# Another list of steps for a kernel of linear attention, a feed-forward layer and a soft mixture of experts

## The chip, the cores and the metric

The kernel runs on one core of one Trainium2 chip. The metric is the device time of one execution in microseconds (us); the median of three runs stands for a kernel. The engines of the core work in parallel: TensorE (PE in the profile; PEld is its loading of weights), VectorE (DVE), ScalarE (ACT), GpSimd (POOL) and SyncE (SP), which issues the DMA transfers. Each goes through its own instructions in order and waits at semaphores for the others.

## What is computed

Three layers follow each other, in fp32. The inputs are 4 batches of 768 tokens with 8 heads of 48 (so 3072 tokens of 384).

```python
# layer 1: linear attention with a decaying state
for t in range(S):
    cur = einsum('bhd,bhe->bhde', u[None] * kt, vt)
    y[:, :, t] = einsum('bhd,bhde->bhe', rt, state + cur)
    state = wt[:, :, :, None] * state + einsum('bhd,bhe->bhde', kt, vt)
# layer 2: x is y as 3072 x 384
h = x @ w_in                      # 384 x 2048
x = (h * cos(h)) @ w_out          # 2048 x 384
# layer 3: soft mixture of 8 experts with 4 slots each
logits = x @ phi                  # 384 x 32
d = softmax(logits, axis=0); slot_input = d.T @ x
for e in range(8):
    slot_out[e] = maximum(slot_input[e] @ w1[e], 0) @ w2[e]
out = softmax(logits, axis=1) @ slot_out
```

## The kernel before

The three layers are not run one after the other. The work is cut into some 1950 steps, and a string, `HEAD` (line 924), lists them by name with their numbers, as `rT.16` or `h.13.1`. A loop at line 710 goes through the string and calls each step's function; inside `manual_schedule` every engine carries out its instructions in the order in which the steps stand in the string. Semaphores see to the data: an engine whose next instruction isn't ready stands still, and everything behind it in its own order too. So the string sets the order on all five engines at once, and nothing else in the kernel does, up to the end of the list. Then a fixed piece of code follows (experts and outputs, lines 711 to 913), which the change leaves alone.

The families of steps that the text speaks of, with their engines and lines:

- **Attention**, 24 blocks of 128 tokens (the number after the name is the block). `lw lk lr lv lz` load on SP. `wT kT rT` transpose on TensorE, four 128x128 transposes each (L145). `wf` copies wT (ACT). `scan`, `sr`, `sp` (DVE, L160, L164, L168) make running products of w. `L` (DVE, L189, two halves) multiplies rT by them into the tile lt, `ks` (DVE, L195) multiplies kT. `kN` (TensorE, L213) transposes ks back, `ksn` (ACT, L236) copies it. `A` (L206) are 16 small matmuls of ks and lt (32 records in the trace: a small fp32 matmul leaves two), `mask` (DVE, L232) takes their half. `U` (L257) are 16 of ksn and v, `st` (DVE, L278) the state. `z` and `rz` scale and place the state, `y` (L289) makes the block's result in 32 small matmuls; `xh`, `xm`, `xc` split it into two parts for the next layer. wT, kT, rT, kN, A, U and y share three PSUM banks in turn, so that U can only be written when the bank that it gets has been read.
- **Feed-forward layer**, 96 units: token block t, quarter q. The weights are decoded in the first 60 us (`raw`, `q`, `abs`, `d2a`, `d2b`, `whi` and others). `h.t.q` is nine matmuls 128x512 on TensorE (L443 to L445). `turns` (ACT, L458), `rest` (DVE, L462), `cos` (ACT, L466) and `mul` (DVE, L471) make h cos(h) from it, in the tile g. It gets transposed by TensorE (`gT`, L478, four transposes, and the copy `gc`, L484) or by DMA (`gz`, `gd`, `gx`). `l.t.q` (L510) multiplies the result by the product of w_out and phi: four small matmuls that add to the logits of a group.
- **Slots**, 12 groups of two token blocks. `sum` and `lc` (TensorE, L523) give the group's logits, `max` (DVE, L531 to L536) their running maximum, `exp xt xr xd` the exponentials (the last group: `quart`, ACT, L542, four copies of a quarter each, and `exp`, ACT, L552), `dT` (L580) transposes them, `dc` (ACT, L587) copies one half into dt and `ltok` (DVE, L593) the other half into the tile ltok. `E.g.p` (L606) multiplies dt by the four g tiles of a token block, a matmul for each (in the last group, whose parts are halves of the columns, eight for each part); it uses the bank in which dT stood. `es` (DVE, L612) adds it to a running sum.
- **Weights of the experts**, 16 transfers of 1.5 MB on SP (`att`, `we`, `late0`).

The decode's and the attention's products need VectorE and ScalarE between two steps on TensorE again and again: rT, then L on VectorE, then A; kN, then ksn on ScalarE, then U; dT, then dc and ltok, then E. Such a way from TensorE to another engine and back is called a hand-over below. In the list, other steps of TensorE stand in between.

Of the kernel before, what the change touches and what calls it, by code (L numbers as in the profile page):

```python
# [928 lines left out]
abs.i.4 wT.2 L.1 d2b.i.4 y.0 q.i.5 d2a.i.5 wf.2 xh.0 kN.1 xm.0 ksn.1 scan.2 U.1 xc.0 lw.3 abs.i.5 st.1.0 h.0.0 d2b.i.5 z.1.1 q.o.0 d2a.o.0 whi.4 A.1
turns.0.0 st.1.1 abs.o.0 D.1 lv.2 rest.0.0 wn.4.0 h.0.1 lz.1 whi.5 rz.1.0 wn.4.1 mask.1 q.i.7 sr.2 raw.o.2 d2b.o.0 sp.2 wc.4.0 kT.2 wn.5.1 cos.0.0  # L930
wc.4.1 rz.1.1 rT.2 wc.5.1 ru.2 raw.o.1 mul.0.0 oT.1 q.i.6 oc.1 ks.2 lk.3 L.2 abs.i.7 wT.3 wn.5.0 d2a.i.7 lr.3 turns.0.1 wf.3 lr.4 wc.5.0 z.2.0 kN.2
ksn.2 d2b.i.7 lk.4 abs.i.6 y.1 xh.1 U.2 d2a.i.6 whi.7 gT.0.0 rest.0.1 st.2.0 scan.3 z.2.1 sr.3 d2b.i.6 xm.1 xc.1 wn.7.0 lv.3 q.o.1 wn.7.1 gc.0.0
cos.0.1 sp.3 wc.7.1 h.1.0 mul.0.1 wc.7.0 abs.o.1 bo.2 rz.2.1 lw.4 abs.o.2 turns.1.0 rT.3 oT.0 d2a.o.1 st.2.1 d2b.o.1 h.0.2 bs.2 oc.0 whi.6 rest.1.0
turns.0.2 raw.o.3 D.2 L.3 A.2 lz.2 q.o.2 wn.6.0 kT.3 mask.2 gT.0.1 wT.4 cos.1.0 rest.0.2 ks.3 wc.6.0 d2a.o.2 lv.4 rz.2.0 wf.4 raw.o.4 mul.1.0 oT.2 y.2
q.o.3 ru.3 xh.2 oc.2 kN.3 xm.2 bo.3 ksn.3 d2b.o.2 A.3 xc.2 oT.3 gc.0.1 oT.5 bs.3 oc.3 D.3 h.1.1 z.3.0 scan.4 d2a.o.3 cos.0.2 abs.o.3 oc.5 lr.5 raw.o.5
wn.6.1 turns.1.1 lw.5 oT.4 oc.4 om.0 mask.3 sr.4 wc.6.1 rest.1.1 rz.3.0 mul.0.2 d2b.o.3 lz.3 abs.o.4 q.o.4 pc.0 U.3 cos.1.1 st.3.0 kT.4 lv.5 h.0.3
ks.4 z.3.1 oT.7 d2a.o.4 oT.6 st.3.1 gT.0.2 oc.7 d2b.o.4 kN.4 oc.6 ksn.4 mul.1.1 rT.4 sp.4 oT.8 om.1 turns.0.3 oc.8 wT.5 abs.o.5 rest.0.3 pT.0 wf.5
ps.0 cos.0.3 h.1.3 q.o.5 pc.1 oT.9 oc.9 turns.1.3 L.4 mul.0.3 d2a.o.5 z.4.0 lw.6 raw.o.7 ru.4 lk.5 U.4 d2b.o.5 st.4.0 gc.0.2 q.o.7 l.0.0 pT.1 rest.1.3
h.1.2 rz.3.1 oT.11 ps.1 gT.0.3 z.4.1 turns.1.2 scan.5 oT.10 oc.11 raw.o.6 rest.1.2 lw.7 bo.4 l.0.1 cos.1.3 ru.5 oc.10 abs.o.7 y.3 st.4.1 om.2 A.4 sr.5
xh.3 wT.6 cos.1.2 gc.0.3 mul.1.3 bs.4 abs.o.6 lz.4 sp.5 D.4 d2a.o.7 h.2.0 gT.1.1 xm.3 q.o.6 mul.1.2 pc.2 d2b.o.7 wf.6 mask.4 h.2.1 oT.14 turns.2.0  # L940
pT.2 gc.1.1 d2a.o.6 rz.4.1 xc.3 oT.15 rz.4.0 ps.2 oc.15 gT.1.0 oc.14 d2b.o.6 close lr.6 l.0.2 rT.5 oT.13 oT.12 gc.1.0 lk.6 gT.1.2 oc.13 bo.5 ru.6
rest.2.0 L.5 cos.2.0 l.1.0 l.1.1 y.4 mul.2.0 oc.12 z.5.0 gc.1.2 xh.4 om.3 kT.5 bo.6 xm.4 pc.3 gT.1.3 pT.3 h.2.2 turns.2.1 lz.5 scan.6 lr.7 rest.2.1
ps.3 sr.6 ks.5 cos.2.1 rT.6 kN.5 gc.1.3 l.1.2 xc.4 sp.6 l.1.3 lz.6 turns.2.2 ksn.5 mul.2.1 L.6 bs.5 l.0.3 sum.0 bs.6 A.5 U.5 rest.2.2 lc.0 rz.5.0 D.5
h.2.3 mask.5 max.0 D.6 gT.2.0 lk.7 st.5.0 lv.6 cos.2.2 exp.0 wT.7 z.5.1 mul.2.2 turns.2.3 kT.6 xt.0 lr.8 xr.0 lw.8 rest.2.3 ks.6 gc.2.0 cos.2.3 st.5.1
mul.2.3 h.3.0 kN.6 xd.0 wf.7 scan.7 h.3.2 turns.3.0 rest.3.0 dT.0 ksn.6 sr.7 U.6 cos.3.0 z.6.0 dc.0 ltok.0 l.2.0 E.0.0 gT.2.1 st.6.0 mul.3.0 rz.5.1
lv.8 lw.9 z.6.1 h.3.1 wT.8 sp.7 turns.3.2 gc.2.1 rest.3.2 ru.7 cos.3.2 turns.3.1 st.6.1 lv.7 mul.3.2 A.6 rest.3.1 mask.6 gT.2.2 h.3.3 gz.3.2 kT.7 wf.8
rz.6.1 l.2.1 cos.3.1 y.5 gz.3.0 gc.2.2 bo.7 bs.7 mul.3.1 rz.6.0 ks.7 gd.3.2 xh.5 rT.7 h.4.1 gd.3.0 xm.5 gz.3.1 lk.8 scan.8 L.7 turns.3.3 sr.8
turns.4.1 xc.5 rT.8 rest.3.3 D.7 kN.7 sp.8 cos.3.3 E.0.1 ksn.7 mul.3.3 rest.4.1 y.6 xh.6 wT.9 wf.9 cos.4.1 h.4.0 L.8 mul.4.1 turns.4.0 xl.6 ru.8
# [115 lines left out]
```

## Time and profile before

| | |
|---|---|
| median of 3 runs (lowest to highest) | 482.76 us (482.46 to 484.51) |
| the profiled execution | 482.29 us, its span 480.5 us |
| busy share: PE, PEld, DVE, ACT, POOL | 94%, 72%, 84%, 74%, 25% |
| mean granted clock of TensorE | 0.993 of full speed |
| chain that ended last: PE, DVE, ACT, DMA | 74%, 11%, 5%, 4% |
| largest group: h matmuls (L443 to L445), 3 x 288 | 121.9 + 112.6 + 113.2 us in records |
| transfers of expert weights (16 of 1.5 MB) | median 9.3 us from issue to landing |

The span runs from the first to the last instruction; 1.8 us of the profiled execution's time lie around it. A busy TensorE isn't TensorE at its peak: matmuls are pipelined and their records overlap, so that the sum of the records of a group can be more than the time that passes. A line of the timeline gives the start, the duration, the engine, the line of the kernel, the operation, the tiles (out<-in) and in brackets the idle time of the engine before it and what ended it. Runs of the same instruction stand in one line with their count; the duration is then that of the run.

### The profile page before, as it was taken

What the parts mean: (1) busy time and instruction counts of PE and PEld (TensorE: products, weight loads), DVE (VectorE), ACT (ScalarE), POOL (GpSimd) and SP (SyncE); (2) the same over time, 40 slices, a digit from 0 to 9 for tenths busy, and PEclk for the clock granted to TensorE, in tenths of its full rate; (3) what the DMA queues carried; (4) which work ended last, traced back from release to release, by engine and by line L of the source; (5) the groups of instructions that cost most, each with busy time, mean ns of one, the idle gap of its engine ahead of it and who ended that gap; (6) DMA issues with size and microseconds to landing.
All of it is one profiled execution on the core that took longest, in us unless ns stands there. A gap on an engine that the chain in (4) does not pass through costs nothing.

```text
span 480.5 us, 15374 instructions
## 1 busy us (share of the span) xinstructions
...
## 2 busy tenths in 40 slices
...
GB/s 214 309 297 211 171 211 208 59 74 84 139 199 127 162 173 139 153 193 172 140 158 158 204 157 177 188 120 149 179 135 130 233 256 411 247 337 405 368 125 272
DMA packets 205589, 94.21 MB, mean 196 GB/s; under 512 B 181840, under 2 KB 187216, under 8 KB 205520
## 3 DMA queue, kind: packets, MB, share of 16 engines
...
## 4 chain that ended last, share of the span: by engine, by line
PE 74%; DVE 11%; ACT 5%; DMA 4%; SPq 3%; issue 1%; POOL 0%; ACTq 0%; POOLq 0%
PE h L443 12%; PE h L445 11%; PE h L444 11%; PE l L510 5%; PE E L606 4%; PE y L289 4%; PE gT L478 4%; PE A L206 3%; PE U L257 3%; PE hps L797 2%; PE so L834 2%; PE wT L145 2%; PE kT L145 2%; DVE g L462 2%; PE rT L145 2%; PE kN L213 2%
## 5 line engine op out<-in xcount | busy, mean ns | idle before, releaser
L443 PE MATMUL h<-wu,x 128*128 128x512 f32 x288 | 121.9, 423 | 0.2
L445 PE MATMUL h<-wu,x 128*128 128x512 f32 x288 | 113.2, 393 | 0.0
L444 PE MATMUL h<-wu,x 128*128 128x512 f32 x288 | 112.6, 391 | 0.0
L466 ACT ACTIVATE g<-g,half_pi 128x512 f32<-128x512 f32 (+1 forms) x97 | 69.5, 720 | 17.0 <-DVE g L462 16.0
L458 ACT ACTIVATE g<-h 128x512 int32<-128x512 f32 (+1 forms) x96 | 57.1, 595 | 32.9 <-PE h L445 25.0
L471 DVE TENSOR_TENSOR g<-g,h 128x512 f32<-128x512 f32 x96 | 64.7, 676 | 9.0 <-ACT g L466 8.1
L462 DVE SCALAR_TENSOR_TENSOR g<-g,h 128x512 f32<-128x512 int32 (+1 forms) x96 | 64.7, 675 | 8.6 <-ACT g L458 7.7
L443 PEld LDWEIGHTS h<-wu,x 128*128 128x128 f32 x288 | 54.3, 189 | 18.2 <-DVE g L471 2.3
L445 PEld LDWEIGHTS h<-wu,x 128*128 128x128 f32 x288 | 54.0, 188 | 12.3
L444 PEld LDWEIGHTS h<-wu,x 128*128 128x128 f32 x288 | 54.4, 189 | 8.7
L220 POOL TENSOR_SCALAR_AFFINE_SELECT lt<-bo 64x512 f32<-64x512 f32 x48 | 38.0, 793 | 68.1 <-ACT bo L248 57.7
L492 ACT COPY zg<-g 128x1024 uint16<-128x1024 uint16 x51 | 52.8, 1042 | 1.8 <-DVE g L471 1.2
L267 POOL TENSOR_TENSOR z<-st_state,qt 128x192 f32<-128x192 f32 x35 | 22.0, 629 | 118.3 <-DVE st_state L278 94.2
L173 POOL TENSOR_TENSOR ru<-rn,u_b 128x384 f32<-128x384 f32 x24 | 26.1, 1086 | 81.5 <-DVE bo L243 32.1
L275 ACT COPY rzs<-z 64x192 f32<-64x192 f32 x96 | 33.4, 348 | 1.4 <-DVE z L263 0.4
L232 DVE COPY_PREDICATED lt<-cs,A 64x256 f32<-64x256 uint32 x72 | 32.2, 447 | 1.9 <-PE A L206 0.4
L189 DVE TENSOR_TENSOR lt<-rT,pt 64x512 f32<-64x512 f32 x48 | 32.8, 684 | 0.8 <-PE rT L145 0.3
L168 DVE TENSOR_TENSOR_SCAN pt<-wf,ini_f 128x520 f32<-128x520 f32 x24 | 30.9, 1289 | 0.0
L160 DVE TENSOR_TENSOR_SCAN qt<-wf,one_b 128x520 f32<-128x520 f32 x24 | 29.8, 1242 | 0.0
L289 PEld LDWEIGHTS y<-lt,rzs 128*32 128x32 f32 x1536 | 23.5, 110 | 6.2 <-issue 3.7
L174 POOL TENSOR_TENSOR ru<-ru,kn 128x384 f32<-128x384 f32 x24 | 26.9, 1120 | 2.0 <-DMA kn<-in_k_dram 0.2
L478 PE MATMUL gT<-cs,g 128*128 128x128 f32 x180 | 27.1, 275 | 0.0
...
## 6 DMA issues: line engine op xcount, KB each, us to landing
...
```

The lines of the kernel that those rows point to most:

```text
L220: nc.gpsimd.affine_select(out=lt[j % 2][h, a], in_=bo_t[j][h, a].unsqueeze(2).to_broadcast([64, NS, C]), pattern=[[0, NS], [-1, C]], compa ...
L275: nc.scalar.copy(rzs[j % 2][64 * a:64 * a + 64, c, :, a, RZ[a]], z_t[j, c][64 * a:64 * a + 64])
L289: nc.tensor.matmul(ps[m:m + 32, o, c * C:(c + 1) * C], lhsT=rz[:, c, p, a, 32 * b:32 * b + 32], rhs=L[:, a, 2 * p + c, :], start=m not in ...
L443: nc.tensor.matmul(half[:, f], lhsT=xh[:, c, :], rhs=wh, start=(c == 0), stop=False)
L444: nc.tensor.matmul(half[:, f], lhsT=xl[:, c, :], rhs=wh, start=False, stop=False)
L445: nc.tensor.matmul(half[:, f], lhsT=xh[:, c, :], rhs=wl, start=False, stop=(c == KD - 1))
L458: nc.scalar.activation(gt.bitcast(I32), hp, AF.Copy, bias=0.25, scale=1.0 / TWO_PI)
L462: nc.vector.scalar_tensor_tensor(out=gt, in0=gt.bitcast(I32), scalar=-TWO_PI, in1=hp, op0=ALU.mult, op1=ALU.add)
L466: nc.scalar.activation(gt, gt, AF.Sin, bias=half_pi[:, 0:1])
L471: (nc.gpsimd if pool else nc.vector).tensor_tensor(out=gt, in0=gt, in1=hp, op=ALU.mult)
L478: nc.tensor.transpose(ps[:, m * 128:(m + 1) * 128], gt[:, m * 128:(m + 1) * 128], ident)
L492: copy(zg, g_t[t, q].bitcast(U16).rearrange("p (f i) -> p i f", i=2))
```

## The change

Only the string `HEAD` differs: the same steps, each as often as before, in another order. No step's code, no tile and no transfer is added, removed or resized; the order of the two engines' accesses to a tile may differ where the steps stand the other way round. The whole of the string's lines is replaced; one of the old and one of the new, from around block 23 of the attention, show what such a line is:

```diff
 HEAD = """
...
-rest.20.1 cos.20.1 cmb.2.2 mul.20.1 rest.20.0 gT.20.1 turns.20.2 kN.23 l.19.0 rest.20.2 l.19.1 l.19.2 z.23.0 ksn.23 cos.20.2 l.19.3 L.23 sum.9 U.23
...
+turns.20.2 gc.19.3 rz.23.0 rT.23 gT.20.1 rest.20.2 l.19.0 l.19.1 ksn.23 rest.20.0 l.19.2 l.19.3 cos.20.2 L.23 U.23 mul.20.2 sum.9 gc.20.1 cos.20.0
...
```

Three places on TensorE, as the two orders have them. In the names, the number behind the last underscore is a tile's running number and means nothing else. A fourth place needs no rows: gT8_3, the transposes of unit (8, 3), stood one h step ahead of dT3 and now stands between dT3 and rT12, so that before E3 come dT3, gT8_3, rT12 and l of unit (8, 0), and in the old list dT3, rT12 and that l.

TensorE before U of attention block 16, at about 264 to 268 us, before and after (nine rows of h13_1 are left out in each but for the first and the last).

```order
L213 MATMUL kN16_4198<-cs_105,ks16_4162 128x128 x4
L145 MATMUL rT16_4214<-cs_105,rn0_119 128x128 x4
L145 MATMUL kT17_4219<-cs_105,kn1_122 128x128 x4
L443 MATMUL h13_1_4237<-wu1_322,x01_116 128x512
...
L445 MATMUL h13_1_4237<-wu1_322,x01_116 128x512
L580 MATMUL dT5_4247<-cs_105,dl1_114 128x128
L257 MATMUL U16_0_4251<-vn0_125,ksn16_4224 64x48
```

```order
L145 MATMUL rT16_4196<-cs_105,rn0_119 128x128 x4
L213 MATMUL kN16_4205<-cs_105,ks16_4179 128x128 x4
L443 MATMUL h13_1_4212<-wu1_323,x01_116 128x512
...
L445 MATMUL h13_1_4212<-wu1_323,x01_116 128x512
L580 MATMUL dT5_4231<-cs_105,dl1_114 128x128
L145 MATMUL kT17_4235<-cs_105,kn1_122 128x128 x4
L257 MATMUL U16_0_4246<-vn0_125,ksn16_4210 64x48
```

kT17 moved from before h13_1 to behind dT5, and rT16 and kN16 changed places.

TensorE at the end of the list, from the last group's logits (lc11) to the second half of its E, before and after.

```order
L523 MATMUL lc11_6715<-lg11_6713,cs_105 128x256
L606 MATMUL E10_6580<-g21_0_6301,dt10_6566 32x512
L606 MATMUL E10_6580<-g21_1_6394,dt10_6566 32x512
L606 MATMUL E10_6580<-g21_2_6280,dt10_6566 32x512
L606 MATMUL E10_6580<-g21_3_6172,dt10_6566 32x512
L580 MATMUL dT11_6743<-cs_105,dl1_114 128x128
L606 MATMUL E11_1_6750<-g22_0_6482,dt11_6745 32x256
```

```order
L523 MATMUL lc11_6714<-lg11_6712,cs_105 128x256
L580 MATMUL dT11_6729<-cs_105,dl1_114 128x128
L606 MATMUL E10_6578<-g21_0_6306,dt10_6567 32x512
L606 MATMUL E10_6578<-g21_1_6330,dt10_6567 32x512
L606 MATMUL E10_6578<-g21_2_6284,dt10_6567 32x512
L606 MATMUL E10_6578<-g21_3_6171,dt10_6567 32x512
L606 MATMUL E11_1_6746<-g22_0_6458,dt11_6736 32x256
```

The second half of E10 moved behind dT11. In the same stretch the steps quart.11 and max.11 (ScalarE and VectorE, both readers of the bank of lc11) changed places in the list.

TensorE before U of attention block 23, at about 384 us, before and after: the rows from the transposes of rT23 to U (h20_2 cut to its first and last row; of U's rows one).

```order
L145 MATMUL rT23_6034<-cs_105,rn1_120 128x128 x4
L443 MATMUL h20_2_6041<-wu2_468,x01_116 128x512
...
L445 MATMUL h20_2_6041<-wu2_468,x01_116 128x512
L510 MATMUL l9_6000<-gx18_2_6039,p_sb_109 32x128 x4
L510 MATMUL l9_6000<-gt18_3_5927,p_sb_109 32x128 x4
L478 MATMUL gT20_1_6075<-cs_105,g20_1_6055 128x128 x4
L213 MATMUL kN23_6082<-cs_105,ks23_6020 128x128 x4
...
L257 MATMUL U23_0_6113<-vn1_126,ksn23_6102 64x48
```

```order
L478 MATMUL gT19_3_6035<-cs_105,g19_3_5857 128x128 x4
L510 MATMUL l9_5951<-gx18_2_6033,p_sb_109 32x128 x4
L510 MATMUL l9_5951<-gt18_3_5993,p_sb_109 32x128 x4
L213 MATMUL kN23_6064<-cs_105,ks23_6001 128x128 x4
L145 MATMUL rT23_6076<-cs_105,rn1_120 128x128 x4
L478 MATMUL gT20_1_6081<-cs_105,g20_1_6046 128x128 x4
...
L257 MATMUL U23_0_6109<-vn1_126,ksn23_6095 64x48
```

rT23 moved from ahead of h20_2 to behind it, behind two l and kN23.

## Rows read from the trace of the kernel before

**Rows 1.** Stretches: length, PE, PEld, DVE, ACT, POOL busy (instructions), PEclk, DMA share, GB/s.

```profile
9.70:60.00 50.30, 44.80 (x549) 31.91 (x549) 48.78 (x73) 44.70 (x83) 14.55 (x14) 1.00 1.03 244
60.00:420.00 360.00, 358.02 (x5030) 279.10 (x5028) 327.26 (x649) 281.78 (x579) 97.79 (x117) 1.00 0.79 171
```

**Rows 2.** Timeline of TensorE at 209 us: start, duration, line, operation, tiles, count.

```profile
209.50 0.60 PE L145 MATMUL wT<-cs,wn 128*128 128x128 f32 x4
210.03 0.69 PE L206 MATMUL A<-lt,ks 64*64 64x64 f32 x32
210.65 0.50 PE L443 MATMUL h<-wu,x 128*128 128x512 f32 x1
210.99 0.40 PE L444 MATMUL h<-wu,x 128*128 128x512 f32 x1
211.22 0.40 PE L445 MATMUL h<-wu,x 128*128 128x512 f32 x1
```

**Rows 3.** Timelines of TensorE and VectorE around U of block 16.

```profile
264.51 0.60 PE L145 MATMUL rT<-cs,rn 128*128 128x128 f32 x4
264.95 0.60 PE L145 MATMUL kT<-cs,kn 128*128 128x128 f32 x4
265.30 0.48 PE L443 MATMUL h<-wu,x 128*128 128x512 f32 x1
...
267.67 0.31 PE L257 MATMUL U<-vn,ksn 64*64 64x48 f32 x2
268.50 0.68 PE L257 MATMUL U<-vn,ksn 64*64 64x48 f32 x30 [0.52 <-DVE lt L189]
269.41 1.07 PE L606 MATMUL E<-g,dt 128*32 128x512 f32 x8 [0.24 <-ACT dt L587]
...
266.97 1.39 DVE L189 TENSOR_TENSOR lt<-rT,pt 64x512 f32<-64x512 f32 x2
```

**Rows 4.** Timeline of TensorE before E of group 3.

```profile
205.58 0.42 PE L510 MATMUL l<-gx,p_sb 128*32 128x128 f32 x8
206.32 1.07 PE L606 MATMUL E<-g,dt 128*32 128x512 f32 x8 [0.31 <-DVE ltok L593]
```

**Rows 5.** Timelines of TensorE and VectorE around U of block 23.

```profile
378.77 0.60 PE L145 MATMUL rT<-cs,rn 128*128 128x128 f32 x4
...
381.38 0.42 PE L510 MATMUL l<-gx,p_sb 128*32 128x128 f32 x8
381.62 0.40 PE L510 MATMUL l<-gt,p_sb 128*32 128x128 f32 x8
...
383.99 1.10 PE L257 MATMUL U<-vn,ksn 64*64 64x48 f32 x32
...
382.98 1.39 DVE L189 TENSOR_TENSOR lt<-rT,pt 64x512 f32<-64x512 f32 x2
```

**Rows 6.** Timeline of VectorE at the start: its second decode step.

```profile
8.94 0.96 DVE L356 SCALAR_TENSOR_TENSOR qi<-rawi,qi 128x768 int32<-128x768 int32 x1 [1.19 <-ACT qi L346]
```

**Rows 7.** Timelines of TensorE, VectorE and ScalarE at the end of the list.

```profile
430.43 0.70 PE L523 MATMUL lc<-lg,cs 128*128 128x256 f32 x2 [0.55 <-DVE lg L517]
431.06 1.06 PE L606 MATMUL E<-g,dt 128*32 128x512 f32 x8
433.44 0.33 PE L580 MATMUL dT<-cs,dl 128*128 128x128 f32 x1 [1.32 <-ACT dl L552]
434.27 1.93 PE L606 MATMUL E<-g,dt 128*32 128x256 f32 x32 [0.51 <-ACT dt L587]
...
432.04 0.42 DVE L531 TENSOR_REDUCE mx<-lc 128x1 f32<-128x256 f32 x1 [1.67 <-ACT dl L542]
...
431.16 0.84 ACT L542 COPY dl<-lc 32x64 f32<-32x64 f32 x4 [0.36 <-PE lc L523]
```

**Rows 8.** Stretches at the end of the list and after the last matmul, columns as in rows 1.

```profile
432.50:433.00 0.50, 0.00 (x0) 0.00 (x0) 0.31 (x2) 0.06 (x1) 0.00 (x0) 1.00 0.99 393
474.25:474.50 0.25, 0.00 (x0) 0.00 (x0) 0.00 (x0) 0.00 (x0) 0.00 (x0) 0.50 1.04 295
```

More of the change, by code (lines that the diff above doesn't have):

```diff
@@ L929 @@
[L929 to L948, printed above, removed]
@@ new lines @@
+y.4 oc.13 om.3 cos.2.0 xh.4 z.6.0 lv.5 mul.2.0 pc.3 scan.6 kT.5 gT.1.2 ks.5 pT.3 bs.5 turns.2.1 ru.6 h.2.2 gc.1.2 lk.7 gT.1.3 rest.2.1 rz.5.0 ps.3
+sr.6 turns.2.2 gc.1.3 lr.7 bo.6 kN.5 rT.6 sp.6 xm.4 D.5 rest.2.2 ksn.5 cos.2.1 l.1.2 l.1.3 l.0.3 L.6 A.5 xc.4 mul.2.1 sum.0 U.5 lv.6 lc.0 mask.5
+cos.2.2 h.2.3 max.0 st.5.0 mul.2.2 exp.0 turns.2.3 gT.2.0 xt.0 rest.2.3 kT.6 gc.2.0 xr.0 xd.0 ks.6 wT.7 h.3.0 gT.2.1 cos.2.3 mul.2.3 lr.8 ru.7 z.5.1
+dT.0 kN.6 wf.7 scan.7 turns.3.0 ksn.6 lk.8 st.5.1 lv.7 ltok.0 h.3.2 dc.0 bs.6 rest.3.0 sr.7 lz.5 U.6 E.0.0 rz.6.0 bo.7 cos.3.0 st.6.0 gc.2.1 mul.3.0
@@ new lines @@
+l.3.2 turns.4.2 rz.7.0 st.7.0 rest.4.2 gz.4.0 cos.4.2 z.7.1 lr.10 l.3.3 scan.9 mul.4.2 lk.10 sum.1 gd.4.1 st.7.1 h.5.0 rz.7.1 z.8.0 ru.10 lc.1 A.8
+kN.8 lz.8 lk.9 turns.5.0 lw.11 max.1 exp.1 rest.5.0 mask.8 ksn.8 cos.5.0 mul.5.0 xt.1 h.4.3 gd.4.0 sr.9 lw.10 xr.1 gz.4.2 gx.4.0 U.8 kT.9 xd.1
+turns.4.3 ks.9 h.5.1 gz.5.0 dT.1 kN.9 rest.4.3 st.8.0 cos.4.3 bo.10 ltok.1 dc.1 y.7 z.8.1 E.1.0 mul.4.3 l.4.0 ru.9 bs.10 xh.7 rz.8.1 st.8.1 lv.9 z.9.0
+wT.10 gd.4.2 turns.5.1 sp.9 gd.5.0 h.5.2 ksn.9 rest.5.1 bo.9 xl.7 wf.10 U.9 cos.5.1 mul.5.1 gT.4.3 rT.9 lw.12 gx.5.0 gx.4.2 st.9.0 turns.5.2 rest.5.2
```

154 lines of the change are left out of this document (83 added, 71 removed).

## The prediction

> **What bounds the kernel now.** I read the stretches first, then TensorE's order in time, then what VectorE and ScalarE did at the places where TensorE stood. The stretches [rows 1]: between 60 and 420 us TensorE is busy for 358.02 of 360.00 us, VectorE for 327.26, ScalarE for 281.78. TensorE bounds this stretch, three quarters of the kernel. Its busy time is not quite its work, however: the records of neighbouring matmuls overlap, so what counts is the distance from one start to the next. Inside an h step (nine matmuls) starts are 0.23 us apart in records of 0.39 to 0.40 us [rows 2], the same wherever I looked. Hence a stall first eats the overlap, unseen, and shows as idle time only afterwards. Going through the starts of 60 to 420 us one by one and comparing each with the usual distance of its kind, I find 9.6 us above the usual, 5.6 us of it at places that lose over 0.15 us each, against 1.98 us of idle time in [rows 1]. That is all that a better order can win there, unless the distances themselves change.
>
> The Trainium skill, page "Perfetto Trace Analysis", section "Identifying the Most-Contended Engine", says that matmul busy time is a poor measure, and that the share of weight loading and the occupancy of the other engines are to be compared. By it TensorE has 279.10 of 360.00 us [rows 1], below VectorE's 327.26, so that VectorE would bound and a list that spares TensorE would bring nothing: the time would stay at 482.8. The even 0.23 us between starts speaks against it here; it stands beside the first rival.
>
> **The change, part by part.** The instructions of each engine are the same; only their order differs.
>
> *Distances.* Four transposes take 0.35 us until an h step starts (264.95 to 265.30), 0.44 until four other transposes (264.51 to 264.95) [rows 3] and 0.53 until small fp32 matmuls such as A (209.50 to 210.03) [rows 2]. An h step takes about 0.10 longer before small matmuls than before transposes (2.25 to 2.27 against 2.16 us, over the 15 such pairs of the trace). Counted in the two lists: transposes before small matmuls 61 to 29 (32 x -0.18 = -5.8 us); transposes before transposes 46 to 67 (21 x +0.09 = +1.9); h before small ones 15 to 44 (29 x +0.10 = +2.9); the other kinds stay within a dozen with distances that are about equal. Sum -1.0 us; with distances as they scatter, -0.6 to -1.4.
>
> *Hand-overs, 60 to 420 us.* Two places show what one costs. E of group 3: TensorE transposes dT, then rT, does an l step at 205.58 and starts E only at 206.32 [rows 4], 0.74 us later, where an l step usually takes 0.24 (381.38 to 381.62 [rows 5]): 0.5 us lost, of which 0.31 are idle. E needs both readers of dT to be done (dt on ScalarE, ltok on VectorE), and only rT and l stand between. The new list puts the four transposes of gT8_3 there too, 0.35 to 0.44 us of work: the loss goes but for about 0.1. U of block 16: it starts at 267.67, stalls 0.52 us for the product lt of VectorE (L189), and E follows at 269.41 [rows 3]; a step of the kind usually takes 0.62 (A, 210.03 to 210.65 [rows 2]), so 1.74 - 0.62 = 1.1 us are lost. Here rT16 was transposed at 264.51, but VectorE came to it at 266.97. So VectorE's queue was late, not TensorE. The new list moves kT17 from before h13_1 to just before U (0.44 us of cover) and takes one 0.2 us reciprocal out of VectorE's queue, but E still waits for the same chain lt, ltok, dt. I count -0.3 of the 1.1 us.
> All places together: with the work on TensorE between a hand-over's two ends minus the time of the middle instruction as cover, 25 of 187 hand-overs of the old list have under 0.5 us, and 13 of 190 of the new one. Half of the 5.6 us would be -2.8; E of group 3 gives back nearly all and U16 a third, so I take -2.0. Ends: 0 (VectorE's queue decides everywhere, as at U16) and -4 (all but the waits on late queues go).
>
> *Start, to 60 us.* VectorE is busy for 48.78 of 50.30 us from 9.7 on, TensorE for 44.80 [rows 1]: VectorE bounds here. The list moves z0 and the second decode step ahead, into the 1.19 us that VectorE stood idle until 8.94 [rows 6]. But the scan that comes next on it needs the first wT from TensorE and wf from ScalarE in any case, so that most of the gain is only moved behind. I take -0.5; ends -2.8 (the VectorE work that the new order takes from before the third token block's first h) and +1.0 (wT1 now stands before kT0 and rT0, so that ks and lt of block 0 come later).
>
> *End, 420 to 437 us.* In the old list ScalarE copies the last logits in four quarters (0.84 us from 431.16), and only then VectorE takes the maximum, at 432.04, though it was idle for 1.67 us [rows 7]; dT follows at 433.44. In the new list the maximum (0.42) goes first and the quarters behind it, while the 0.3 us of VectorE that follow the maximum run beside them: dT about 0.45 us earlier. But E10's second half (1.06 us, 431.06), which filled the wait for dT, now stands behind dT, where it fills the 0.83 us from dT to E11 (433.44 to 434.27) and overruns it by a few tenths. Together -0.1; ends -0.5 and +0.4.
>
> *Weights.* The transfers of expert weights (16 of 1.5 MB, 9.3 us from issue to landing by the table) stand in both lists in nearly the same place, the last five in another sequence. I cost it at 0, since the output stage uses them one after the other and none is due at once; without that cover the one that is moved to the end would be late by up to the fifth of 9.3 us that five of them share out, +2.
>
> Sum: -1.0 - 2.0 - 0.5 - 0.1 = -3.6 us on the profiled execution's 482.29 us: 478.7. The profiled execution lies 0.47 below the median of the runs shown (482.76), so the forecast is **479.2 us**. This kernel's measurement can tell about 0.5%, 2.4 us, from no change: faster is below 480.35, slower above 485.2.
>
> **Rivals.**
> 1. *The hand-overs bring nothing*, because VectorE's queue, not TensorE's list, is late wherever TensorE stands, as at U16 (lt 2.5 us after its rT started [rows 3]). Then the distances, 1.0 us, are all: 482.76 - 1.0 = 481.8. For it: VectorE busy 327.26 of 360 [rows 1]. Against: E of group 3.
> 2. *VectorE's queue before lt: slower.* The new list transposes rT later. Block 23 is the clearest place: rT was at 378.77, lt at 382.98, U at 383.99 [rows 5]; now rT stands behind h, l and kN, 1.3 us of TensorE's work before U, less than the 1.39 us of the two halves of lt alone. Seven blocks have under 0.9 us of cover before the one that needs lt or its bank, three before. If VectorE is not free just then, each waits for its queue: U16 shows 1.9 us from the end of rT (264.51 + 0.60) to lt; less about 0.5 of cover, 1.4 us each. Four more such places: +5.6, and the hand-overs' -2.0 are then not there either: -1.6 + 5.6 = +4.0, **486.8**. It decides from three places on (+2.6). Against: at block 23 VectorE reached lt at 382.98 anyway, about when the new rT ends, and the old list's three places lost some 0.3 us in all.
> 3. *The clock falls at the end.* Between the last logits and dT TensorE stood idle for 1.32 us and kept the granted clock of 1.00, 2.4 GHz (row of 432.50 to 433.00) [rows 7, 8]. Without E10 in between it stands about 1.9 us. After its very last matmul the row of 474.25 to 474.50 has 0.50, 1.2 GHz, with no matmul in it [rows 8]. If the clock falls, E10's half and E11 (1.06 + 1.93 us [rows 7]) take up to twice as long: +2.5, so 481.7.
> 4. *The start follows VectorE wholly* (-2.8 instead of -0.5): 476.9.
> 5. *Weights late* by 2 us: 481.2.
>
> The Trainium skill, page "TensorE: Matmul & The Clock Gate", part 1, has the clock released by recent activity and gated after idleness; the rows at the end agree, and it is the third rival's mechanism. The rows of 431 to 434 us show that an idle stretch nearly as long left the clock alone, so the rival stays a rival.
>
> **How the numbers follow.** Forecast (479.2, itself 477 to 481) 0.40; rival 1 0.17; rival 2 0.17; rival 3 0.12; rival 4 0.09; rival 5 0.05. Faster by over 0.5%: rival 4 and all of the forecast but the sixth that lies above 480.35, 0.43. Slower: rival 2, 0.17. The same: the rest, 0.40. The range leaves out a tenth on either side: low 475.5, since the ends of the middle (-4), the distances (-1.4) and the start (-2.8) hardly come together; high 485.5, within rival 2.
>
> **What would show it.** In the changed profile: the start of the last dT minus the start of the last logits, 2.6 us instead of 3.0, with quarters behind the maximum; E of group 3 starting without idle time; U16's stall still there but under 0.5 us; TensorE's idle time from 60 to 420 us under 1.5 us, and that stretch of work some 3 us shorter. Rival 2 shows as TensorE waiting for lt (L189) at blocks 3, 6, 10 and 23; rival 3 as a granted clock below 1.00 around 435 us and E11 records of 3 us and more. I am wrong if the sum of TensorE's waits in the middle grows, or if an h step follows another by over 2.16 us where nothing is idle.

## The result, and the profile after

The changed kernel takes 490.4 us (median of 4 runs, 488.35 to 491.4) against 482.66 us for the kernel before: 1.0141 times as long, with a 95% interval of 1.0116 to 1.0166. The forecast was 479.2 us and faster. Its profiled execution has a span of 489.1 us, 8.6 more than before.

Three readings of TensorE split these 8.6 us: the start of the first group's logits, of the last group's, and of the column sums behind the last E (all lc at L523, the sums at L765).

| | before | after | difference |
|---|---|---|---|
| first logits | 100.91 | 105.59 | +4.7 |
| from the first to the last logits | 329.52 | 331.06 | +1.5 |
| from the last logits to the column sums | 5.92 | 8.25 | +2.3 |
| from there to the end of the span | 44.15 | 44.20 | 0.0 |

So in this execution the start loses most, the middle, where the gain was to come from, loses too, and the end loses as much as a rival had said. One execution is one draw, however. The experiments below leave parts of the list as they are, and their profiled executions show how far such a reading goes without any change. The end of the new list took 5.59 to 8.25 us in seven kernels, its middle 329.91 to 332.18 us in eight, and its first logits came at 104.69 to 105.70 us in four. The old list's end took 5.92 us in three kernels and its middle 329.52 to 329.88 us in five.

The stretches of the kernel after, columns as in [rows 1]:

```profile
9.70:60.00 50.30, 42.16 (x470) 30.62 (x471) 46.83 (x66) 40.47 (x77) 14.64 (x14) 1.00 1.06 247
60.00:420.00 360.00, 356.48 (x5069) 275.85 (x5068) 326.16 (x635) 281.73 (x577) 94.15 (x117) 1.00 0.77 164
57.00:58.00 1.00, 0.00 (x0) 0.00 (x0) 0.94 (x3) 0.45 (x1) 0.90 (x1) 1.00 0.86 332
60.00:61.00 1.00, 1.00 (x6) 1.00 (x5) 0.00 (x0) 0.75 (x2) 0.00 (x0) 0.50 0.11 29
438.00:439.00 1.00, 0.00 (x0) 0.00 (x0) 0.42 (x3) 0.93 (x6) 0.00 (x0) 0.73 0.87 296
440.00:441.00 1.00, 1.00 (x8) 0.20 (x4) 0.45 (x2) 0.14 (x1) 0.00 (x0) 0.50 1.00 406
```

The first row stands against 44.80 us of TensorE in [rows 1], 549 matmul records against 470: the same stretch does less. The third and the fourth are one event: TensorE idle for a whole microsecond, and then busy at a granted clock of 0.50, that is 1.2 GHz. The last two are another of the same kind.

**The end.** Timelines of TensorE, VectorE and ScalarE, against [rows 7]:

```profile
436.65 0.70 PE L523 MATMUL lc<-lg,cs 128*128 128x256 f32 x2 [0.55 <-DVE lg L517]
439.21 0.47 PE L580 MATMUL dT<-cs,dl 128*128 128x128 f32 x1 [1.87 <-ACT dl L552]
439.62 5.35 PE L606 MATMUL E<-g,dt 128*32 128x512 f32 x40
444.90 0.56 PE L765 MATMUL sum<-st_s,cs 128*128 128x1 f32 x2
...
437.38 0.42 DVE L531 TENSOR_REDUCE mx<-lc 128x1 f32<-128x256 f32 x1 [0.79 <-PE lc L523]
...
437.84 0.84 ACT L542 COPY dl<-lc 32x64 f32<-32x64 f32 x4 [0.81 <-DVE mx L531]
```

The maximum goes first and the quarters follow, as worked out: from the logits to dT 2.56 us instead of 3.01. But without E10 in between TensorE is idle for 1.87 us, and E10's half and E11 take 5.35 us, where before they took 1.06 and 1.93.

**Two places at the start.** First the beginning, TensorE:

```profile
9.94 2.27 PE L145 MATMUL wT<-cs,wn 128*128 128x128 f32 x8 [9.94 <-DMA cs<-in_const_dram]
12.23 1.11 PE L145 MATMUL kT<-cs,kn 128*128 128x128 f32 x4
13.14 1.06 PE L145 MATMUL rT<-cs,rn 128*128 128x128 f32 x4
15.32 1.11 PE L213 MATMUL kN<-cs,ks 128*128 128x128 f32 x4 [1.11 <-ACT wf L155]
17.29 1.68 PE L385 MATMUL wl<-ai,cs 128*128 128x512 f32 x2
19.13 0.68 PE L257 MATMUL U<-vn,ksn 64*64 64x48 f32 x32
```

Four transposes take 1.06 to 1.11 us here, against 0.60 in [rows 2]: half pace, though the granted clock of this stretch reads 1.00. That reading says nothing. The trace has no record of the clock before 18.61 us (before 13.31 us in the kernel before), and a stretch without a record reads 1.00. In the kernel before four transposes had come down to 0.74 us by 13.05 and U.0 ran at 17.79; here kN, at 15.32, still has 1.11.

Then the place at 56 us, TensorE, VectorE and GpSimd:

```profile
55.50 0.49 PE L397 MATMUL woT<-cs,wo_sb 128*128 128x128 f32 x3
58.61 1.16 PE L385 MATMUL wl<-ai,cs 128*128 128x512 f32 x2 [2.62 <-DVE lt L228]
59.99 1.06 PE L478 MATMUL gT<-cs,g 128*128 128x128 f32 x4
60.84 1.06 PE L145 MATMUL kT<-cs,kn 128*128 128x128 f32 x4
...
53.94 1.38 DVE L189 TENSOR_TENSOR lt<-rT,pt 64x512 f32<-64x512 f32 x2
55.36 1.69 DVE L361 SCALAR_TENSOR_TENSOR wo_sb<-wo_sb,qo 128x768 int32<-128x768 int32 x1
57.08 1.48 DVE L228 COPY_PREDICATED lt<-cs,A 64x512 f32<-64x512 uint32 x2
...
53.79 1.47 POOL L220 TENSOR_SCALAR_AFFINE_SELECT lt<-bo 64x512 f32<-64x512 f32 x2 [11.04 <-ACT bo L248]
```

The decode matmul wl waits 2.62 us for the mask of block 2 (L228), though it has nothing to do with attention: the bank that it gets is the one in which A.2 stands, and only the mask reads A.2. The new list does A.2 five steps of TensorE earlier (ahead of wn.7.0, h.1.0, wn.7.1, rT.3 and h.0.2), so that it holds the bank from 47.8 us on; the mask can't come before GpSimd has written its tile (until 55.26) and stands behind lt and a decode step on VectorE. Behind the wait, gT and kT take 1.06 us each, at a granted clock of 0.50.

A wait of the same kind stands at 25 us, TensorE and VectorE:

```profile
27.19 0.67 PE L385 MATMUL wl<-ai,cs 128*128 128x256 f32 x2 [2.15 <-DVE lt L228]
...
23.13 2.40 DVE L361 SCALAR_TENSOR_TENSOR ai<-ai,qi 128x768 int32<-128x768 int32 x1 [0.24 <-ACT ai L340]
```

Here too a decode matmul waits for a mask, and the mask stands behind a decode step of VectorE. That step takes 2.40 us, where the one at 20.68 takes 0.96; why is open. The kernel before never stands there for over 0.6 us. No experiment below is about this place; with all four repairs the wait is 0.73 us.

**The middle.** E of group 3, against [rows 4], with VectorE and ScalarE:

```profile
211.00 0.43 PE L510 MATMUL l<-gx,p_sb 128*32 128x128 f32 x8
212.06 1.06 PE L606 MATMUL E<-g,dt 128*32 128x512 f32 x8 [0.63 <-ACT dt L587]
...
211.03 0.47 DVE L593 COPY ltok<-dT 64x64 f32<-64x64 f32 x2
...
211.59 0.42 ACT L587 COPY dt<-dT 64x64 f32<-64x64 f32 x2 [0.88 <-DVE ltok L593]
```

From l to E it takes 1.06 us, against 0.74 before, although gT8_3 now stands in between. ltok comes first, at 211.03, when VectorE gets to it, and ScalarE, idle for 0.88 us, reads the other half of the same bank only when that is done. In none of the 12 groups of either trace do the two copies overlap: the one that stands second in the list starts after the first has ended. In the old list dc stood first in the groups 0, 2, 3, 4 and 8; the new list has ltok first in all five.

### The profile page after: what moved, and what is told of

Same layout as the page of the kernel before. It is cut to its first block, busy times and chain, and to the rows that moved or that the text cites. A ratio compares the mean times of both kernels' runs of the same rounds, so it can differ in the third digit from the quotient of the medians.

```text
span 489.1 us, 15382 instructions
## 1 busy us (share of the span) xinstructions
PE 456.8 (93%) x6313; PEld 346.2 (71%) x6313; DVE 406.8 (83%) x783; ACT 354.9 (73%) x727; POOL 118.8 (24%) x162
## 4 chain that ended last, share of the span: by engine, by line
PE 67%; DVE 17%; issue 6%; ACT 5%; DMA 2%; POOL 1%; SPq 0%; ACTq 0%; POOLq 0%; DVEq 0%
PE h L443 11%; PE h L445 10%; PE h L444 10%; PE E L606 5%; PE l L510 4%; PE gT L478 3%; PE y L289 3%; PE hps L797 2%; PE so L834 2%; DVE g L462 2%; PE U L257 2%; PE A L206 2%; PE wT L145 2%; DVE lt L232 2%; DVE g L471 2%
## 5 line engine op out<-in xcount | busy, mean ns | idle before, releaser
L471 DVE TENSOR_TENSOR g<-g,h 128x512 f32<-128x512 f32 (+1 forms) x96 | 64.7, 674 | 5.2 <-ACT g L466 4.2
L220 POOL TENSOR_SCALAR_AFFINE_SELECT lt<-bo 64x512 f32<-64x512 f32 x48 | 34.9, 727 | 86.1 <-ACT bo L248 48.3
L267 POOL TENSOR_TENSOR z<-st_state,qt 128x192 f32<-128x192 f32 x35 | 23.3, 667 | 103.3 <-DVE st_state L278 79.1
L173 POOL TENSOR_TENSOR ru<-rn,u_b 128x384 f32<-128x384 f32 x24 | 24.4, 1016 | 84.4 <-DMA rn<-in_r_dram 52.0
L189 DVE TENSOR_TENSOR lt<-rT,pt 64x512 f32<-64x512 f32 x48 | 32.9, 684 | 0.9 <-PE rT L145 0.5
L168 DVE TENSOR_TENSOR_SCAN pt<-wf,ini_f 128x520 f32<-128x520 f32 x24 | 31.9, 1328 | 0.1
L606 PE MATMUL E<-g,dt 128*32 128x512 f32 (+1 forms) x208 | 27.6, 624 | 2.3 <-ACT dt L587 2.1
```

The lines of the kernel that those rows point to most:

```text
L220: nc.gpsimd.affine_select(out=lt[j % 2][h, a], in_=bo_t[j][h, a].unsqueeze(2).to_broadcast([64, NS, C]), pattern=[[0, NS], [-1, C]], compa ...
L471: (nc.gpsimd if pool else nc.vector).tensor_tensor(out=gt, in0=gt, in1=hp, op=ALU.mult)
L606: nc.tensor.matmul(ps[32 * q:32 * q + 32, cols], lhsT=dt_[:, tt, :], rhs=g_t[2 * g + tt, q][:, cols], start=(tt == 0), stop=(tt == 1))
```

## The experiments

Each is a list with one or a few steps moved, or with matmuls added that nobody reads. Ratios are to the kernel before in runs beside them; that of the new list is 1.0141 (1.0116 to 1.0166).

**The end.** The second half of E10 goes back.

```diff
-... lc.11 max.11 quart.11 exp.11 dT.11 E.10.1 cmb.2.6 ...
+... lc.11 max.11 quart.11 exp.11 E.10.1 dT.11 cmb.2.6 ...
```

> The new list, with one step moved: the second half of E10 stands before dT11 again (the maximum stays ahead of the quarters). Theory 'the clock falls': TensorE no longer stands idle for 1.87 us between the last logits and dT, the granted clock stays at 1.00 around 438 to 445 us, and the last E takes some 2 us instead of being part of 5.35; from the start of the last logits to the column sums 5.6 us instead of 8.25, so 490.4 - 2.6 = 487.8. Rival 'E10 only overruns': the clock is not the cause, E10's 1.06 us is only moved behind dT; at most 0.6 us comes back, 489.8.

487.15 us, ratio 1.0085 (1.006 to 1.011): 3.2 us less than the new list. From the last logits to the column sums it takes 5.49 us (435.06 to 440.55), 2.8 us less, with TensorE idle for 0.88 us. The theory's size; the rival allowed 0.6. (The first logits, too, are 0.9 us earlier in this execution, where nothing was changed.) This does not yet tell the clock from the order, since E10 moved. The next adds work and moves nothing:

```diff
+ def warm(n):
+     ps = ps_t.tile([128, 512], F32, tag="t", name="warm")
+     for i in range(n):
+         nc.tensor.transpose(ps[:, 0:128], ident, ident)
...
-... quart.11 exp.11 dT.11 E.10.1 ...
+... quart.11 exp.11 warm.14 dT.11 E.10.1 ...
```

> The new list, unchanged, with 14 transposes of the identity added on TensorE between the last logits and dT11; nobody reads their bank. They add work and take none away. Theory 'the clock falls' (the price of the end is the granted clock): TensorE is busy in the gap, the clock stays at 1.00, and E10's half and E11 take some 3 us instead of 5.35; the time falls by 2.3 to 488.1. Rival 'E10 behind dT costs': added transposes can't bring anything, 490.4 or a little more.

486.81 us, ratio 1.0076 (1.0055 to 1.0097). Its timeline of TensorE:

```profile
434.80 0.70 PE L523 MATMUL lc<-lg,cs 128*128 128x256 f32 x2 [0.55 <-DVE lg L517]
435.34 1.69 PE L665 MATMUL warm<-cs 128*128 128x128 f32 x14
437.37 0.33 PE L580 MATMUL dT<-cs,dl 128*128 128x128 f32 x1 [0.34 <-ACT dl L552]
437.63 2.79 PE L606 MATMUL E<-g,dt 128*32 128x512 f32 x40
440.38 0.35 PE L770 MATMUL sum<-st_s,cs 128*128 128x1 f32 x2
```

The same 40 records of E take 2.79 us instead of 5.35, in the same order, at a granted clock of 1.00 instead of 0.50. From the logits to the sums it takes 5.58 us, 0.1 more than with E10 in its old place: behind dT, E10 costs next to nothing by itself. These 2.7 us are the theory's; the rest of the 3.6 lies where the two lists are the same.

Six kernels below leave this part of the new list as it is, and TensorE is idle for the same 1.87 us in each. They show that the clock, and not the order, stretches E: its 40 records take 5.35 us in one of them, 4.36 to 4.48 us in four, whose clock was at 0.50 for a shorter time, and 2.79 us in the one (wn.0.1 moved, see the beginning) whose clock stayed at 1.00:

```profile
440.17 0.33 PE L580 MATMUL dT<-cs,dl 128*128 128x128 f32 x1 [1.87 <-ACT dl L552]
440.43 2.79 PE L606 MATMUL E<-g,dt 128*32 128x512 f32 x40
```

With the new list's own, the same wait lowered the clock in six executions of seven. So one execution with the 14 transposes can't show by itself that they kept it up. What speaks for them is that the clock fell behind no wait of 0.7 to 1.4 us in any of the traces (the last section has the counts). From the other side, the old list with E10's half moved:

```diff
-... lc.11 quart.11 late0 E.10.1 we.8 max.11 exp.11 dT.11 dc.11 ...
+... lc.11 quart.11 late0 we.8 max.11 exp.11 dT.11 E.10.1 dc.11 ...
```

> The old list with one step moved: the second half of E10 stands behind dT11, as in the new list (the quarters stay ahead of the maximum, so that TensorE is idle for some 2.3 us between the last logits and dT11). Theory 'the clock falls': a granted clock of 0.50 at E10 and E11, +2.6 us, about 485.5 to 486. Rival 'no clock': E10's half fills the 0.8 us wait for E11, +0.3.

484.98 us, ratio 1.0029 (1.0013 to 1.0044): slower, by about 1.5 us rather than 2.6. Timeline and a stretch:

```profile
433.32 0.33 PE L580 MATMUL dT<-cs,dl 128*128 128x128 f32 x1 [2.31 <-ACT dl L552]
433.58 4.48 PE L606 MATMUL E<-g,dt 128*32 128x512 f32 x40
```

```profile
435.00:436.00 1.00, 1.00 (x13) 0.43 (x8) 0.88 (x2) 0.00 (x0) 0.00 (x0) 0.50 1.03 415
```

Here the idle 2.31 us were longer, but dT still ran in 0.33 us, and the clock fell only after it: a part of E was done before. So the price isn't a fixed one; it depends on whether and when the clock falls and how much work comes before it is back.

**The maximum before the quarters**, in the old list alone:

```diff
-... lc.11 quart.11 late0 E.10.1 we.8 max.11 exp.11 ...
+... lc.11 max.11 quart.11 late0 E.10.1 we.8 exp.11 ...
```

> The old list with one step moved: max.11 ahead of quart.11, as in the new list (E10 stays before dT11). Theory 'two readers of one bank': VectorE needn't wait for the four quarters; from the last logits to the column sums 5.5 us instead of 5.92, 0.4 us less in all, 483.0 beside 483.4. Rival: ScalarE's quarters come later by the same 0.4 us, no change.

482.47 us, ratio 0.997 (0.9953 to 0.9988). From the logits to the sums it takes 5.48 us (431.05 to 436.53) instead of 5.92: the 0.44 us that the prediction worked out for the new list's end. The interval lies wholly under 1; it is the one version here that is clearly under the kernel before, and it is one step of the new list. The ratio is worth some 1.4 us; the trace shows 0.44 us of it.

**The place at 56 us.**

```diff
-... xc.1 A.2 rest.0.1 wn.7.0 ... h.0.2 wc.7.1 L.3 rz.2.0 ... wn.6.0 ...
+... xc.1 rest.0.1 wn.7.0 ... h.0.2 wc.7.1 L.3 A.2 rz.2.0 ... wn.6.0 ...
```

> The new list, with one step moved: A.2 stands behind L.3 as in the old list, not before wn.7.0. Theory 'a bank held': A.2 takes its bank later, the decode matmuls of wn.6.0 get another bank and don't wait 2.62 us for VectorE's mask at 56 to 58.6 us, the granted clock stays at 1.00 from 59 to 63 us, and 3.3 us come back: 487.1. Rival 'VectorE is late anyway': the mask comes at the same time, whoever is next for the bank waits for it instead, and under 1 us comes back: 489.6.

486.79 us, ratio 1.0077 (1.0054 to 1.01): 3.6 us less, and the first logits are at 102.4 instead of 105.59. Timeline of TensorE and VectorE:

```profile
55.73 1.02 PE L385 MATMUL wl<-ai,cs 128*128 128x512 f32 x2
56.82 0.60 PE L478 MATMUL gT<-cs,g 128*128 128x128 f32 x4
58.55 0.63 PE L145 MATMUL kT<-cs,kn 128*128 128x128 f32 x4 [1.13 <-issue]
...
56.96 1.49 DVE L228 COPY_PREDICATED lt<-cs,A 64x512 f32<-64x512 uint32 x2
```

The mask comes when it came (56.96 against 57.08), but nobody needs A.2's bank in the meantime: wl runs at 55.73. kT waits instead, for 1.13 us, and after that wait four transposes take 0.63 us, not 1.06. How much of the loss was the wait and how much the clock, the next kernel separates; it leaves the order as it is:

```diff
-... lk.4 D.2 wn.6.0 gT.0.1 ...
+... lk.4 D.2 warm.18 wn.6.0 gT.0.1 ...
```

> The new list, unchanged, with 18 transposes of the identity added on TensorE ahead of wn.6.0, into the gap of 2.62 us at 56 to 58.6 us in which TensorE waits for VectorE's mask; nobody reads their bank. Theory 'the wait costs twice': the mask still comes when it came, but the granted clock stays at 1.00 from 59 to 63 us, and the work there takes half the time: the first logits 1.5 us earlier, 488.9. Rival 'the wait alone costs': the first logits at the same time, 490.4.

488.88 us, ratio 1.0098 (1.0069 to 1.0126). Timeline of TensorE:

```profile
56.04 2.13 PE L665 MATMUL warm<-cs 128*128 128x128 f32 x18
58.83 1.13 PE L385 MATMUL wl<-ai,cs 128*128 128x512 f32 x2 [0.67 <-DVE lt L228]
60.46 0.60 PE L145 MATMUL kT<-cs,kn 128*128 128x128 f32 x4
```

wl can't start earlier (58.83), kT takes 0.60 instead of 1.06, and A of block 3 starts at 63.66 instead of 64.95, although wl was 0.2 later. So at this place the clock's part is 1.5 us. In this execution the first logits are only 0.2 us earlier: at 98.0 us TensorE stands for 0.63 us between two matmuls of one step, for a reason that the profile doesn't name. The median's 1.5 us, with intervals that overlap, can't settle how much stays. Other kernels can. The wait of some 2.6 us also stands in those with E10's half moved back, with 14 transposes, with the old first steps and with four matmuls at the start (the last two below), but the clock stayed at 1.00 behind it: from the end of the wait to the first logits they take 45.6 us. The new list and the two others in which it fell to 0.50 (wn.0.1 moved, dc first) take 47.0. So the clock's part is 1.4 us at the first logits, all of which stays, and the wait brought it in three of seven executions.

**The beginning.** One step first:

```diff
-... wf.1 q.i.3 kN.0 wn.0.1 L.0 ...
+... wf.1 q.i.3 wn.0.1 kN.0 L.0 ...
```

> The new list, with one step moved: wn.0.1 (three decode matmuls) stands before kN.0, as in the old list. Theory 'TensorE warms late': the 1.11 us idle before kN.0 shrink, matmuls have their full pace from about 14 us on instead of 18.5, U.0 starts 1.2 us earlier (about 17.9), and the time falls to about 489.2. Rival 'VectorE bounds the start': U.0 may be earlier, but the mask of block 0 on VectorE is not, and at the logits of group 0 nothing is left: 490.4.

489.32 us, ratio 1.0122 (1.0095 to 1.0149), not to be told from the new list's. U.0 ran at 19.21, no earlier than 19.13: the theory fell in this form. wn.0.1 now waited 1.07 us itself, for wf, because the bank that it got was that of wT.1. The step was not late by its place, but by its bank. Next the old list's first 38 steps, with the new order behind them:

> The new list, its first 38 steps replaced by the old list's first 38 steps (up to kN.0); all others follow in the new order. Theory 'a bank at the start': with wT.1 behind rT.0 and ks.0 ahead of sp.0 the decode matmul wn.0.1 finds a free bank at 13.8 us and TensorE gets to full pace by 16 us; U.0 is 1.3 us earlier than in the new list (17.8), and 1.2 us stay: 489.2. Rival 'VectorE bounds the start': the mask of block 0 comes no earlier, 490.4.

487.39 us, ratio 1.0074 (1.005 to 1.0098): 3.0 us less, more than the 1.2 expected. U.0 ran at 18.05, the first logits at 103.15, 2.4 earlier. Of these, 1.0 us are there when the wait at 56 us ends (wl at 57.60 instead of 58.61), and 1.4 us are the fall of the clock behind it, which didn't come here. Pace or order? The following kernel keeps the new list and puts four matmuls of a constant tile on TensorE before its first operand is there:

```diff
+ def heat(n):
+     ps = ps_t.tile([128, 512], F32, tag="t", name="heat")
+     for i in range(n):
+         nc.tensor.matmul(ps[:, 0:512], lhsT=one_b[:, 0:128], rhs=one_b[:, 0:512], start=True, stop=True)
...
-z.0.0 raw.i.1 rz.0.0 ...
+heat.4 z.0.0 raw.i.1 rz.0.0 ...
```

> The new list, with four matmuls 128x512 of a constant tile added on TensorE at 4 us, about 5 us of work, done before the first operand comes at 9.9 us. Theory 'TensorE warms late': full pace at 10 us, U.0 at 17.9 instead of 19.13, the first logits 1 to 2 us earlier, 489. Rival 'order': wn.0.1 and kN.0 wait for wf.1 and ks.0 as before, U.0 at 18.8 or later and the first logits unmoved, 490.4.

Timeline of TensorE:

```profile
3.98 6.04 PE L665 MATMUL heat<-one_b 128*128 128x512 f32 x8 [3.98 <-POOL one_b L661]
9.85 0.60 PE L145 MATMUL wT<-cs,wn 128*128 128x128 f32 x4
17.99 0.68 PE L257 MATMUL U<-vn,ksn 64*64 64x48 f32 x32 [0.64 <-ACT ksn L236]
```

Full pace from the first transpose, and U.0 at 17.99 in the new order: nearly all of its delay against the kernel before (17.79) is the pace, not the order. The first logits are at 102.97, 2.6 us earlier. Again 1.2 us of it are there when the wait at 56 us ends (wl at 57.41), and 1.4 us are the fall of the clock that didn't come. The time doesn't confirm it as clearly: 489.02 us, ratio 1.013 (1.01 to 1.016), overlaps the new list's, and 1.0 us of the 2.6 was lost again by the last logits, nearly all at U of 168.9 us, which waits 0.97 us for the load of v.

Nor does the order settle the pace. Full pace (the first record of the clock) begins at 13.8 and 14.1 us in two kernels whose first steps are the new list's, those of the end with E10's half moved back and with 14 transposes; U.0 ran at 18.36 and 18.52 there. It begins at 18.2 to 19.0 us in the five others with the new list's first steps or wn.0.1 moved, and at 13.3 to 15.6 us in all six with the old ones and no added matmuls ahead. In the old list the pace is worth nothing:

> The old list with the same four added matmuls at 4 us. Theory 'TensorE warms late': wf.0 0.6 us earlier, 0.5 us less in all, 482.8 beside 483.3. Rival 'VectorE bounds the start': the scan at 11.7 can't be earlier, no change.

483.3 us, ratio 1.0011 (0.9991 to 1.0032); U.0 at 17.90, the first logits at 100.59 against 100.91. The old list already gets its full pace in time, and there VectorE bounds. A first try with six matmuls had overrun:

> The old list, with six matmuls 128x512 of a constant tile added on TensorE from about 4 us on, before its first operand is there at 9.8 us; nobody reads their bank. Theory 'TensorE warms late': the transposes at 9.8 to 13 us take 0.44 us apart instead of 1.1, wf.0 comes 0.6 us earlier; some 1 us less, 482.4. Rival 'VectorE bounds the start': its scan at 11.70 follows a decode step that ends then anyway; U.0 and the first logits move by under 0.3 us, no change.

484.68 us, ratio 1.0027 (1.0004 to 1.0051). A 128x512 matmul of fp32 took some 1.3 us on average, twice what I had assumed; the six ended at 11.4, wT.0 started 1.6 us late, and VectorE's scan stood idle for 1.06 us. It tells nothing of the pace, but shows that the start hangs on wT.0.

**The readers of dT's bank.** In the groups 0, 2, 3, 4 and 8 dc goes ahead of ltok again, as in:

```diff
-... ltok.3 ... dc.3 ... E.3.0 ...
+... dc.3 ltok.3 ... E.3.0 ...
```

> The new list, with the copies dc ahead of ltok again in groups 0, 2, 3, 4 and 8, as in the old list (in the new one ltok on VectorE reads the bank of dT first). Theory 'two readers of one bank': E of groups 2, 3 and 4 no longer stands for dt (2.1 us of waits in all), E of group 3 loses under 0.3 us instead of 0.84, and the time falls by 1.5 to 488.9. Rival 'the order of the two does not matter', since E needs both: the waits only change their name to ltok, 490.4.

488.58 us, ratio 1.0108 (1.008 to 1.0135); the interval overlaps the new list's. The trace is clearer: E's waits for dt from 76 to 418 us fall from 2.1 to 0.3 us (at group 5, left with ltok first), with 0.2 for ltok, and from the first to the last logits it takes 329.57 us instead of 331.06. The waits for dt are 1.5 to 2.1 us in all eight kernels with the new list's middle and at most 0.3 in the four with dc first; the middle takes 329.91 to 332.18 us in the eight and 328.95 to 330.44 in the four, so that the length of a single one tells less than the waits. At group 3, ScalarE, VectorE and TensorE:

```profile
209.82 0.40 ACT L587 COPY dt<-dT 64x64 f32<-64x64 f32 x2
...
210.26 0.47 DVE L593 COPY ltok<-dT 64x64 f32<-64x64 f32 x2
...
210.87 1.07 PE L606 MATMUL E<-g,dt 128*32 128x512 f32 x8 [0.21 <-DVE ltok L593]
```

dc fills the time until VectorE is free, and E follows ltok at once, 0.64 us after l (210.23) instead of 1.06.

**All four repairs together**: the old first 38 steps, A.2 behind L.3, dc first in every group, E10's half before dT11.

> The new list with all four repairs: its first 38 steps from the old list, A.2 behind L.3, dc ahead of ltok in every group, E10's second half before dT11. If the four losses are separate, the times add: 490.4 - 1.2 - 3.6 - 1.6 - 2.9 = 481.1, a little under the old list's 482.7 to 483.7, by the distances (-0.6) and the smaller stall at U16. Rival 'what is saved at the start and in A.2 is the same wait': 483 to 484.

482.46 us, ratio 0.9987 (0.9971 to 1.0004): 7.9 us less than the new list, no different from the kernel before. First logits at 100.86, last at 429.81, column sums at 435.28: against the kernel before 0.0, -0.6 and -0.4 more. So the four places account for the whole loss. One by one the repairs had brought 3.2, 3.6, 3.0 and 1.8 us by their medians, 11.6 us in all, so they overlap. The fall of the clock at 59 us, for one, is missing in the profiled executions of three of the four, and can be saved only once. With added matmuls at the start:

> The new list with all four repairs, and the six added matmuls at the start. If the start gains 1 us by them, 481.4; if VectorE bounds the start, 482.4 as without them.

> The new list with all four repairs and the four added matmuls. With the old list's first steps in it, the start is VectorE's: no change beside a_all, 482.4; if TensorE's pace counts, 481.9.

484.94 us (1.0024, 1.0003 to 1.0045; the six matmuls overran here too) and 482.86 us (0.9984, 0.9964 to 1.0004): with four no change, as where VectorE bounds.

**The old list with what looked good in the new one:**

```diff
-... gT.8.3 ... h.9.1 ... dT.3 rT.12 gc.8.3 ...
+... h.9.1 ... dT.3 gT.8.3 rT.12 gc.8.3 ...
...
-... lc.11 quart.11 late0 E.10.1 we.8 max.11 ...
+... lc.11 max.11 quart.11 late0 E.10.1 we.8 ...
```

> The old list with max.11 ahead of quart.11, dc ahead of ltok in all groups (three of them, 1, 5 and 10, had it the other way round) and gT.8.3 between dT.3 and E.3.0 as in the new list. Theory 'readers and cover': E of group 3 loses 0.2 instead of 0.5 us, E of group 5 0.4 less, the end 0.4: 482.3 beside 483.3. Rival: VectorE's queue takes it all back but for the end, 482.9.

483.74 us, ratio 1.0002 (0.9984 to 1.0021): worse than with the maximum alone. Three things were moved at once here, so the time tells none of them; the trace does for one. E of group 3 lost more, not less. TensorE and ScalarE:

```profile
206.40 0.43 PE L510 MATMUL l<-gx,p_sb 128*32 128x128 f32 x8
208.23 1.06 PE L606 MATMUL E<-g,dt 128*32 128x512 f32 x8 [1.40 <-DVE ltok L593]
...
206.07 0.59 ACT L484 COPY gt<-gT 128x512 f32<-128x512 f32 x1 [1.06 <-PE gT L478]
207.17 0.41 ACT L587 COPY dt<-dT 64x64 f32<-64x64 f32 x2
```

gT8_3 was moved, its copy on ScalarE was not. ScalarE stood for 1.06 us for the transposes that now came later, and dc, behind it, was at 207.17. The 0.44 us that the move gave as cover on TensorE it took more than back on ScalarE.

## Why the prediction was wrong, point by point

- **The distances: -1.0, estimated -0.6 from the traces.** Summing each kind's usual distance (the lowest quarter of its distances) over the 405 steps of TensorE from about 72 to 418 us gives 330.9 us for the old order and 330.3 for the new. The size hangs on what is called usual: over the starts from the first to the last logits, with all profiled kernels pooled by the kinds of a step and of the one behind it, the lowest quarter gives -1.6 and the median +0.2. The term was small; more isn't shown.
- **The hand-overs: -2.0, measured +1.5 in this execution, with the distances in it.** E's waits for dt and ltok alone grew by that, from 0.55 to 2.08 us. This step failed, and so did the sign that the prediction had set for it: TensorE's idle time from 60 to 420 us grew from 1.98 to 3.52 us. It counted as cover the work on TensorE between the two ends, and took the middle instruction at its own duration. dT has two readers on two engines, and here the one that stands second in the list always waited for the first. If the first stands in VectorE's long queue, ScalarE's idle time is of no use. I had the numbers for E of group 3 and the order of the two steps before me, and did not look which of them came first. With dc first again, the middle is as long as before (329.57 against 329.52), so that what this order was to win isn't there either. U16 went better than forecast: from U to E it took 1.03 us (274.00 to 275.03) instead of 1.74, -0.7 rather than -0.3.
- **The start: -0.5 with ends -2.8 and +1.0, measured +4.7.** The step failed by both its parts. It looked for what VectorE does earlier, since VectorE bounds there, and took TensorE's order as cheap. With the new first steps TensorE stood at half pace until 18.6 us instead of 13.3, which cost 1.0 to 1.2 us. I had seen that the transposes take 1.1 us at first and did not ask what ends that. And A.2, five steps earlier, held one of three banks from 47.8 us until the mask had run, at 58.6: with A.2 moved back the first logits were 3.2 us earlier, 1.4 of it because the clock didn't fall behind the wait. So pace, wait and fall are some 1.1, 1.8 and 1.4 us of the 4.7; what the wait at 25 us costs is open. The pace and the fall are in part luck: other executions with the same steps had full pace by 14 us, or no fall at 59 us.
- **The end: -0.1, measured +2.3 in this execution.** The first half was right to a hundredth: dT 0.45 us earlier (2.56 against 3.01, and 0.44 in the old list with that one step). The second half was the third rival: 2.5 us were worked out, 2.33 came. That the size fits so well is luck: the seven kernels with this end lost between -0.3 and +2.3 us by it, 1.3 in the middle of them. It had the place, the idle time of 1.9 us (1.87) and the mechanism, and was given a chance of 0.12, because an idle stretch of 1.32 us had left the clock alone. That row spoke for 1.32 us and for nothing longer. The other row, 0.50 after the last matmul, was the only one on what happens when TensorE stands longer, and it should have weighed more.
- **Weights: 0, measured 0.** From the column sums to the end the two executions differ by 0.05 us.
- **The second rival**, VectorE's queue before lt, did not come. U of block 23 stood no longer than before, and lt of L189 is not among the waits of the middle. The prediction's own argument against it was right: at block 23 VectorE comes to lt (389.29) only after the later rT has ended (389.04). Its name was right and its place wrong: the queue that cost was VectorE's, at the mask and at ltok.
- **The first rival and the rule** by which VectorE alone bounds: the middle did not stay the same, since it got longer by waits of TensorE for ScalarE, with VectorE's 326.16 us as they were. The three places that cost most lie where TensorE was idle, or slow after it. The Trainium skill, page "TensorE: Matmul & The Clock Gate", part 1, has idleness as what gates the clock. The traces agree in that the clock fell only behind the longest waits, and the same 40 records of E took 5.35 us after such a fall and 2.79 us without one; but the same wait did not always bring it.
- **The range** ended at 485.5, and its chances had one bad case at a time. The measured 490.4 lies beyond it, because start, middle and end were wrong in one direction at once. A list of 1950 steps that is wholly new has many places like these, and I had looked at four.
